# Even steps for a float64 conversion, split weight loads and another order of quad weights in an attention + two-MoE kernel on one core

## The chip, the cores and the metric

One core of one Trainium2 chip runs the whole program. The metric is the device time of one execution in microseconds (us); of several executions the median counts. Before the change three runs gave 1294.26, 1291.40 and 1289.12 us, median 1291.4 us.

## What is computed

Three layers, all in float32 (the weights of the last one come in as float64):

```python
k_p, v_p = mean over 8 keys of k, v                  # 72 pooled keys per head
x = softmax(q @ k_p.T / 8) @ v_p                     # 4 x 8 heads, 576 queries, 64 wide
x = x as (2304, 512)
out = sum over e < 4 of p[:, e] * (relu(x @ w1[e]) @ w2[e])          # w1: 512 x 1024
xn = out / rms(out) * rms_g
y = (silu(xn @ w_gate) * (xn @ w_val)) @ w_out       # 512 x 1536, 1536 x 512, float64 in
```

Every product is built from three fp32r matmuls: each operand is split into a high part (a copy rounded to fp32r) and a low part (the rest), and high x high, high x low and low x high are summed. Over 2 x 2 blocks the products use seven block products instead of eight, so weights and activations need sums and differences of blocks too.

## The kernel before

**Quads.** The unit of work is a *quad*: `quad` (L431) makes four 128-row blocks of hidden values for 768 tokens. It has seven steps (`STEPS`), each of 6 matmuls 128x384 on banks qX, qY, qZ (L462 to L464). After most steps ScalarE copies a bank out (`s`, L470, or `qZ`, L467) or VectorE adds one to `u` (L472, L474). Bank qX is used by steps 0, 2, 4 and 6: step 2 waits for the copy `qZ` after step 0, step 4 for the copy `s` after step 2, step 6 for `u` (L474) after step 4.

**Stages.** There are three passes of 16 MoE quads (kind `m`), then three passes of 12 gate/value quads (kinds `g` and `v` in turn). In this document quad 0 is the first MoE quad, quad 47 the last, quad 48 the first gate quad. The second MoE product (`second`, matmuls 128x512 into `py`, L787 to L789) and the output product (`gx`, `gy`) are threaded between the steps as units.

**The hook.** After each step `hook(n, ...)` is called with the step's number and emits, in this order: the evacuations, the side units, one piece of the next quad's weight preparation (`prep_w`), activations for the next stage (`next_x_ops`), `tick()`, and one step of the background conversion (`next(bg[0])`) unless attention work takes this hook. Everything is emitted in program order into in-order queues (the schedule is manual), so an instruction that waits holds up all that stands behind it on its engine. All DMAs but a few at the start are issued from SP's queue.

**Puts.** `put(dst, src)` (L234) does not issue a store at once: it is issued by the `tick` two hooks later.

**Weights of a quad.** In the first pass over a layer's weights `load_w` (L244) loads the raw blocks into tag `rw` (value quads: `rw2`), and `prep_w` (L254) makes `wr` (three raw blocks, high and low) and `wt` (four sums) with POOL, ScalarE and VectorE, and stores both to DRAM. In later passes `prep_w` only loads `wr` (768 KB) and `wt` (1024 KB) back, L264 and L265, at hook 0 of the quad before. Steps 0, 5 and 6 use `wr` (step 0 only its first block), steps 1 to 4 `wt`. All tags have one buffer unless said otherwise. Tag `rw2` is also the home of the tile `xt` (`xr["s2"]`), which the last quads of MoE pass 3 need for the activations of the first gate pass; its last reader is L207.

**Conversion.** `convert_all` (L326) runs in MoE passes 2 and 3 as the background task: 36 pieces of 128x512 float64 values are loaded as two words each (`cr`), turned into float32 by six VectorE integer operations (`ca`, L367 to L376), one ScalarE copy (`cx`, L369) and two POOL operations (L378, L379), and stored to `wc_d` (24 gate and value pieces) or, for `w_out`, two pieces at a time, combined into eight operands (`combine`, L383) and stored to `ws_d`. `cx` alternates between tag `rw2` and a buffer of the attention pool (`vr`), `cr` between `rw` and `kr`; the two integer arrays `a` and `m` are one tile on tag `tw`. `halt[0]` stops it in the last four quads of a pass.

The places that the prediction's steps touch: `prep_w` around the boundary of quads 47, 48 and 49; the body of `convert_all`; L264/L265.

Of the kernel before, what the change touches and what calls it, by code (L numbers as in the profile page):

```python
# [26 lines left out]
P = 128  # L27
# [11 lines left out]
G = 2  # L39
# [15 lines left out]
def tile_kernel(ctx: ExitStack, tc, qp, kp, vp, dp, w1r, w2r, w64, rg, out):  # L55
    nc = tc.nc
    ctx.enter_context(tc.manual_schedule())
    main = ctx.enter_context(tc.tile_pool(name="main", bufs=1))
    dram = ctx.enter_context(tc.tile_pool(name="dram", bufs=1, space=bass.MemoryType.DRAM))

    def f32(ap):
        return ap.bitcast(F32)
# [169 lines left out]
    puts, clock = [], [0]  # L232

    def put(dst, src):  # L234
        puts.append((clock[0] + 2, dst, src))
# [8 lines left out]
    def load_w(i):  # L244
        if i >= NQ or quads[i][1]:
            return
        k, p, e, r = quads[i]
        t = main.tile([P, 4, 256], F32, name="rw", tag="rw2" if k == "v" else "rw")
        src = w1r[e, r] if k == "m" else wc_d[KINDS.index(k), r]
        nc.sync.dma_start(t.rearrange("p s n -> p (s n)"), src)  # L250
        raw[i] = t

    def prep_w(i):
# [27 lines left out]
        if k == "m":  # L281
            load_w(i + 1)
# [43 lines left out]
    def convert_all():  # L326
# [17 lines left out]
        load(0)  # L344
        yield True
        yield True
        for n, (k, r_, c) in enumerate(keys):
            stop = halt[0]
            if n not in crs:
                load(n)  # L350
                yield True
# [12 lines left out]
            if k < 2:  # L364
                yield True
# [4 lines left out]
            nc.vector.scalar_tensor_tensor(a, hw, 0x80000000, a, op0=ALU.bitwise_and, op1=ALU.bitwise_or)  # L370
            yield True

            mi = m.bitcast(I32)
            nc.vector.tensor_scalar(mi, mi, float(897 << 20), -1.0, op0=ALU.is_ge, op1=ALU.mult)
            nc.vector.scalar_tensor_tensor(a, a, 0x40000000, m, op0=ALU.bitwise_xor, op1=ALU.bitwise_and)
            nc.vector.tensor_scalar(m, a, 0xFF800000, None, op0=ALU.bitwise_and)  # L376

            nc.gpsimd.tensor_tensor(x, x, m.bitcast(F32), op=ALU.mult)  # L378
            nc.gpsimd.tensor_tensor(x, a.bitcast(F32), x, op=ALU.add)  # L379
            if k < 2:  # L380
                put(wc_d[k, r_, :, c * 512:(c + 1) * 512], x)
            else:
                halves[c] = x  # L383
                spare[c] = xt[:, 512:].bitcast(F32R).rearrange("p (a n) -> p a n", a=2)
                if c:
                    yield from combine(r_, halves, spare)
            yield not stop

    def combine(r, halves, spare):
# [12 lines left out]
        def high(t, src):  # L402
            nc.scalar.activation(t[:, 0], src, AF.Copy)

        def low(t, src, n):
            nc.vector.tensor_tensor(t[:, 1], src, f32(t[:, 0]), op=ALU.subtract)
            put(ws_d[r // G, n // 2, :, n % 2, r % G], f32(t))
# [16 lines left out]
        high(t[2], src[2])  # L424
        yield True
        low(t[2], src[2], 2)
        high(t[3], src[3])
        high(t[4], src[4])
        yield True
        low(t[3], src[3], 3)  # L430
        low(t[4], src[4], 4)  # L431
        high(t[6], src[6])
        yield True
        low(t[6], src[6], 6)
# [767 lines left out]
    for si, ((moe, p), ids) in enumerate(stages):  # L1202
# [3 lines left out]
        for i in ids:  # L1206
# [6 lines left out]
            def hook(n, u, v, x):  # L1213
# [18 lines left out]
                halt[0] = i in ids[-4:]  # L1232
# [107 lines left out]
```

## Time and profile before

| | |
|---|---|
| median of three runs | 1291.4 us (1289.12 to 1294.26) |
| the profiled execution, its own time | 1290.88 us |
| its span, first to last instruction | 1289.0 us |
| PE busy / PE weight load busy | 1250.3 us (97%) / 1154.3 us (90%) |
| VectorE / ScalarE / POOL busy | 814.9 / 534.8 / 269.2 us |
| DMA traffic | 339.15 MB, 263 GB/s mean |

The profile says of each engine how long it worked and, before an instruction that started after a pause, what ended the pause. Matmuls are pipelined, so "busy" of PE includes their overlap; the start-to-start distance of two matmuls tells the rate. The span is 1.9 us shorter than the execution's own time.

### The profile page before, as it was taken

The numbers are of one execution on the slowest core, as the hardware profiler recorded it, in microseconds if no ns is written. First come the engines' busy times: TensorE is split into PE (matmuls) and PEld (weight loads), VectorE is DVE, ScalarE is ACT, GpSimd is POOL, SyncE is SP. The second block draws the span as 40 slices with busy tenths as digits, with TensorE's granted clock in tenths as the row PEclk, the third lists the DMA queues.
The fourth block names the chain that finished last, engine by engine and source line by source line (L and its number), as shares of the span: only waits on it lengthen the run. The fifth ranks groups of instructions, "written<-read, shape, count | busy, mean of one in ns | idle before, by whom it ended". The sixth has DMA issues, their size and how long they took to land. (4 is left out here: it accounts for less than half of the span.)

```text
span 1289.0 us, 18313 instructions
## 1 busy us (share of the span) xinstructions
PE 1250.3 (97%) x6872; PEld 1154.3 (90%) x6872; DVE 814.9 (63%) x1340; ACT 534.8 (41%) x1239; POOL 269.2 (21%) x253
## 2 busy tenths in 40 slices
PE   7899999999999999999999999989999999999998
PEld 6788888889888898888988898878999999999998
DVE  5865565557466566544777786465667765786575
ACT  5664444444453333323433342254554433433331
POOL 5335333410032222100342432022220000000000
PEclk8899999999999999999999999989999999999999
DMA  8297777868877777564888997647877776867571
GB/s 245 85 341 275 273 255 257 296 218 322 304 252 283 284 282 266 212 237 175 338 289 313 346 332 264 268 172 257 335 262 276 272 294 234 316 239 303 218 281 50
DMA packets 96537, 339.15 MB, mean 263 GB/s; under 512 B 9408, under 2 KB 32960, under 8 KB 77248
## 3 DMA queue, kind: packets, MB, share of 16 engines
q1 hardware_dynamic: 96112, 336.80, 71.5%
q10 hardware_dynamic: 336, 1.18, 0.3%
q8 instruction: 54, 0.88, 0.3%
q14 instruction: 35, 0.29, 0.1%
HBM read 233.61 MB, written 104.33 MB: 262 GB/s over the span
## 5 line engine op out<-in xcount | busy, mean ns | idle before, releaser
L799 DVE SCALAR_TENSOR_TENSOR y<-py,dps,y 128x512 f32<-128x512 f32 x126 | 94.4, 749 | 183.9 <-PE py L789 183.7
L378 POOL TENSOR_TENSOR cx<-cx,ca 128x512 f32<-128x512 f32 x36 | 48.9, 1357 | 379.1 <-DVE ca L376 127.7
L462 PE MATMUL qX<-xos,wt 128*128 128x384 f32 x336 | 116.9, 348 | 10.4 <-ACT s L470 7.7
L464 PE MATMUL qX<-xos,wt 128*128 128x384 f32 x336 | 114.1, 339 | 0.0
L463 PE MATMUL qX<-xos,wt 128*128 128x384 f32 x336 | 113.7, 338 | 0.0
L789 PE MATMUL py<-w,hB 128*128 128x512 f32 x288 | 113.5, 394 | 0.0
L789 PE MATMUL py<-w,hA 128*128 128x512 f32 x288 | 113.4, 394 | 0.0
L788 PE MATMUL py<-w,hB 128*128 128x512 f32 x288 | 113.3, 393 | 0.0
L788 PE MATMUL py<-w,hA 128*128 128x512 f32 x288 | 113.2, 393 | 0.0
L787 PE MATMUL py<-w,hB 128*128 128x512 f32 x288 | 112.1, 389 | 0.3 <-DVE y L799 0.3
L787 PE MATMUL py<-w,hA 128*128 128x512 f32 x288 | 112.0, 389 | 0.0
L491 ACT ACTIVATE hB<-u 128x768 fp32r<-128x768 f32 x48 | 40.8, 849 | 138.1 <-DVE u L474 138.0
L271 POOL TENSOR_TENSOR tw<-rw 128x512 f32<-128x512 f32 x28 | 40.6, 1449 | 274.7 <-DVE wt L289 173.5
L470 ACT ACTIVATE s<-qX 128x384 f32<-128x384 f32 x85 | 41.6, 489 | 115.0 <-PE qX L464 114.9
L467 ACT ACTIVATE qZ<-qX 128x384 f32<-128x384 f32 x83 | 39.8, 480 | 117.1 <-PE qX L464 83.2
L472 DVE TENSOR_TENSOR u<-qY,s 128x384 f32<-128x384 f32 x84 | 46.6, 554 | 64.3 <-PE qY L464 30.6
L462 PEld LDWEIGHTS qX<-xos,wt 128*128 128x128 f32 x336 | 63.6, 189 | 18.9 <-ACT s L470 10.0
L463 PEld LDWEIGHTS qX<-xos,wt 128*128 128x128 f32 x336 | 63.7, 190 | 2.9
L789 PEld LDWEIGHTS py<-w,hB 128*128 128x128 f32 x288 | 54.0, 188 | 11.5
L789 PEld LDWEIGHTS py<-w,hA 128*128 128x128 f32 x288 | 54.0, 188 | 11.4
L464 PEld LDWEIGHTS qX<-xos,wt 128*128 128x128 f32 x336 | 63.6, 189 | 0.2 <-DVE wt L289 0.2
L787 PEld LDWEIGHTS py<-w,hB 128*128 128x128 f32 x288 | 54.1, 188 | 10.3 <-DVE y L799 0.7
(188 smaller groups left out, 3487.4 us busy)
## 6 DMA issues: line engine op xcount, KB each, us to landing
wt<-wt_d SPq DMA_DIRECT2D x56, 1024.0 KB, 8.2
wr<-wr_d SPq DMA_DIRECT2D x56, 768.0 KB, 6.3
w<-w_d SPq DMA_DIRECT2D x32, 1024.0 KB, 9.3
wt_d<-wt SPq DMA_DIRECT2D x28, 1024.0 KB, 7.3
wr_d<-wr SPq DMA_DIRECT2D x28, 768.0 KB, 5.8
cr<-w SPq DMA_DIRECT2D x36, 512.0 KB, 5.4
w<-ws_d SPq DMA_DIRECT2D x18, 1024.0 KB, 5.4
w_d<-w SPq DMA_DIRECT2D x16, 1024.0 KB, 10.5
```

Of the source, the lines that this page charges most:

```text
L271: nc.gpsimd.tensor_tensor(t[:, T1:N3 + 1], r[:, B12:B12 + 1].to_broadcast([P, 2, 256]), r[:, B11:B22 + 1], op=sub)
L378: nc.gpsimd.tensor_tensor(x, x, m.bitcast(F32), op=ALU.mult)
L462: nc.tensor.matmul(bank[b], wh, xh, start=first and k == 0, stop=False, **kw)
L463: nc.tensor.matmul(bank[b], wh, xl, start=False, stop=False, **kw)
L464: nc.tensor.matmul(bank[b], wl, xh, start=False, stop=k == 1, **kw)
L470: nc.scalar.activation(s[n], bank[b], AF.Copy)
L472: nc.vector.tensor_tensor(u[:, 0], bank["Y"], s[2], op=ALU.add)
L491: nc.scalar.activation(h[:, 0], u, AF.Relu)
L787: nc.tensor.matmul(ps, lhs[0], w[:, 0, c], start=j == 0, stop=False)
L788: nc.tensor.matmul(ps, lhs[0], w[:, 1, c], start=False, stop=False)
L789: nc.tensor.matmul(ps, lhs[1], w[:, 0, c], start=False, stop=j == len(units) - 1)
L799: nc.vector.scalar_tensor_tensor(y_t[t], ps, gate, y_t[t], op0=ALU.mult, op1=ALU.add)
```

## The change

It has four parts. (1) In `convert_all` the work of a piece is spread over three steps with two VectorE operations each; the integer array `a` alternates between tag `tw` and a new buffer `ca` of the attention pool, and `m` moves into the unused half of the piece's `cx` tile; the next load into a buffer is emitted at the end of the piece that read it (`load(n + 2)`), with two loads at a start; the stores of converted data wait three hooks instead of two. (2) In `combine` the same operations stand in six parts instead of seven. (3) In later passes `wr` is loaded as two DMAs, its first block before `wt` and the other two behind it. (4) Value quads keep their raw weights in `rw` and gate quads but the first in `rw2`, and around the first gate quad the load of quad 49 is emitted after quad 48's L279 instead of at the end of its preparation. The conversion is halted half a quad later.

```diff
-    def put(dst, src):
-        puts.append((clock[0] + 2, dst, src))
+    def put(dst, src, steps=2):
+        puts.append((clock[0] + steps, dst, src))
...
-        t = main.tile([P, 4, 256], F32, name="rw", tag="rw2" if k == "v" else "rw")
+        t = main.tile([P, 4, 256], F32, name="rw", tag="rw2" if k == "g" and r else "rw")
...
-            nc.sync.dma_start(wrf, wr_d[n])
+            d = wr_d[n].rearrange("p (a s n) -> p a s n", a=2, s=3)
+            nc.sync.dma_start(f32(wr)[:, :, :1], d[:, :, :1])
             nc.sync.dma_start(wtf, wt_d[n])
+            nc.sync.dma_start(f32(wr)[:, :, 1:], d[:, :, 1:])
...
-        if k == "m":
+        if k == "m" or quads[i - 1][0] == "m":
             load_w(i + 1)
...
         if k != "m":
-            if quads[i - 1][0] == "m":
-                load_w(i + 1)
             load_w(i + 2)
...
-            if not stop:
-                load(n + 1)
             r = crs.pop(n)
             lw, hw = r[:, :, 0], r[:, :, 1]
-            am = main.tile([P, 2, 512], U32, name="ca", tag="tw")
-            a, m = am[:, 0], am[:, 1]
             if n % 2:
+                a = sba.tile([P, 512], U32, name="ca", tag="ca")
                 xt = sba.tile([P, 1024], F32, name="cx", tag="vr")
             else:
+                a = main.tile([P, 1024], U32, name="ca", tag="tw")[:, :512]
                 xt = main.tile([P, 1024], F32, name="cx", tag="rw2")
-            x = xt[:, :512]
-            if k < 2:
-                yield True
+            x, rest = xt[:, :512], xt[:, 512:]
+            m = rest.bitcast(U32)
...
+            if not halt[0]:
+                load(n + 2)
             if k < 2:
-                put(wc_d[k, r_, :, c * 512:(c + 1) * 512], x)
+                put(wc_d[k, r_, :, c * 512:(c + 1) * 512], x, 3)
...
-            yield not stop
+            yield n + 1 in crs
...
-                halt[0] = i in ids[-4:]
+                halt[0] = i in ids[-3:] or i == ids[-4] and n >= 3
```

Three places where instructions move. First SP's queue at the boundary from the MoE to the gate quads; `rw<-wc_d` are raw weights of gate and value quads, in the order of quads 48, 49, 50 and on, `wr_d`/`wt_d<-` the stores of prepared weights. Before:

```order
L250 DMA rw_7490<-wc_d_73 128x1024
L315 DMA w2_7523<-w2_d_76 128x2048
L315 DMA w2_7644<-w2_d_76 128x2048
L241 DMA wr_d_74<-wr_7588 128x1536
L250 DMA rw_7725<-wc_d_73 128x1024
L250 DMA rw_7727<-wc_d_73 128x1024
L241 DMA wt_d_75<-wt_7589 128x2048
L241 DMA wr_d_74<-wr_7740 128x1536
```

The same place in the changed kernel:

```order
L250 DMA rw_7522<-wc_d_73 128x1024
L315 DMA w2_7555<-w2_d_76 128x2048
L315 DMA w2_7676<-w2_d_76 128x2048
L250 DMA rw_7702<-wc_d_73 128x1024
L241 DMA wr_d_74<-wr_7620 128x1536
L250 DMA rw_7759<-wc_d_73 128x1024
L241 DMA wt_d_75<-wt_7621 128x2048
L241 DMA wr_d_74<-wr_7772 128x1536
```

Quad 49's load (the second `rw`) has moved ahead of quad 48's store of `wr` and no longer stands beside quad 50's; quad 50's keeps its place.

Second, VectorE's queue in quad 28, the last conversion pieces of pass 2 (`sm`, `es` are attention). Before:

```order
L990 TENSOR_TENSOR es_4503<-es_4503,sm_4502 128x576
L799 SCALAR_TENSOR_TENSOR y_3298<-py_4597,dps_70,y_3298 128x512
L367 TENSOR_SCALAR ca_4614<-cr_4526 128x512
L368 TENSOR_SCALAR ca_4614<-cr_4526 128x512
L370 SCALAR_TENSOR_TENSOR ca_4614<-cr_4526,ca_4614 128x512
L472 TENSOR_TENSOR u_4571<-qY_4588,s2_4622 128x384
L799 SCALAR_TENSOR_TENSOR y_3298<-py_4637,dps_70,y_3298 128x512
L374 TENSOR_SCALAR ca_4614<-ca_4614 128x512
```

The same place in the changed kernel:

```order
L990 TENSOR_TENSOR es_4516<-es_4516,sm_4515 128x576
L799 SCALAR_TENSOR_TENSOR y_3305<-py_4611,dps_70,y_3305 128x512
L365 TENSOR_SCALAR ca_4625<-cr_4486 128x512
L366 TENSOR_SCALAR cx_4626<-cr_4486 128x512
L370 SCALAR_TENSOR_TENSOR ca_4625<-cr_4486,ca_4625 128x512
L372 TENSOR_SCALAR cx_4626<-cx_4626 128x512
L472 TENSOR_TENSOR u_4584<-qY_4602,s2_4636 128x384
L799 SCALAR_TENSOR_TENSOR y_3305<-py_4650,dps_70,y_3305 128x512
```

The order around `u` is nearly the same; `ca` and `cx` are now buffers that the piece before does not use, and the second operation writes into `cx`.

Third, SP's queue in MoE pass 3, where the first two pieces of `w_out` are combined (`ws_d` stores; `yl`, `xs_d` belong to the norm; `w2` are MoE weights). Before:

```order
L241 DMA ws_d_77<-oh_6042 128x512
L341 DMA cr_6181<-w64 128x1024
L241 DMA ws_d_77<-oh_6044 128x512
L837 DMA yl_6218<-y_d_78 128x512
L341 DMA cr_6234<-w64 128x1024
```

In the changed kernel, where `cr_6048` is the load of the piece that `cr_6181` holds above, and `cr_5978` that of the piece before it:

```order
L341 DMA cr_5978<-w64 128x1024
L265 DMA wr_6005<-wr_d_74 128x2x256
L266 DMA wt_6006<-wt_d_75 128x2048
L267 DMA wr_6005<-wr_d_74 128x2x512
L837 DMA yl_6042<-y_d_78 128x512
L341 DMA cr_6048<-w64 128x1024
L315 DMA w2_6069<-w2_d_76 128x2048
L88 DMA xs_d_72<-st_6040 256x1x128 x2
L241 DMA ws_d_77<-cx_5935 128x512
```

The raw piece is requested ahead of the stores of the pieces before it, a whole group of stores earlier, and each load of `wr` is two.

## Rows read from the trace of the kernel before

**Rows 1.** The page's engine row, and the granted clock in 40 slices (tenths).
```profile
PE 1250.3 (97%) x6872; PEld 1154.3 (90%) x6872; DVE 814.9 (63%) x1340; ACT 534.8 (41%) x1239; POOL 269.2 (21%) x253
...
PEclk8899999999999999999999999989999999999999
```

**Rows 2.** PE's instructions in order of time around the first gate quad: start, duration, instruction, [idle before <-releaser].
```profile
853.65 0.34 PE L464 MATMUL qY<-xoa,wt 128*128 128x384 f32 x1
859.09 0.69 PE L462 MATMUL qX<-xos,wt 128*128 128x384 f32 x1 [5.10 <-ACT s L470]
859.57 0.53 PE L463 MATMUL qX<-xos,wt 128*128 128x384 f32 x1
859.89 0.53 PE L464 MATMUL qX<-xos,wt 128*128 128x384 f32 x1
...
862.77 0.41 PE L464 MATMUL qZ<-xoa,wr 128*128 128x384 f32 x1
...
864.58 0.33 PE L462 MATMUL qX<-xoa,wr 128*128 128x384 f32 x1
864.75 0.33 PE L463 MATMUL qX<-xoa,wr 128*128 128x384 f32 x1
```

**Rows 3.** The same stretch on SP, ACT and DVE.
```profile
839.23 0.95 DVE L279 TENSOR_TENSOR wr<-rw,wr 128x768 fp32r<-128x768 f32 x1
...
852.35 0.96 DVE L207 TENSOR_TENSOR xr<-xr,xt 128x768 f32<-128x768 f32 x1
853.37 0.80 SPq L250 DMA_DIRECT2D rw<-wc_d  x2
857.08 0.84 ACT L277 ACTIVATE wr<-rw 128x768 fp32r<-128x768 f32 x1 [5.13 <-DMA rw<-wc_d]
857.83 0.83 ACT L170 ACTIVATE xos<-xr 128x768 fp32r<-128x768 f32 x1
858.57 0.47 ACT L470 ACTIVATE s<-qX 128x384 f32<-128x384 f32 x1
```

**Rows 4.** Windows: length, PE, PEld, DVE, ACT, POOL busy (instructions), granted clock, DMA share, GB/s.
```profile
858.00:860.00 2.00, 0.91 (x3) 0.91 (x4) 2.00 (x2) 1.98 (x4) 1.84 (x3) 0.50 0.97 401
```

**Rows 5.** PE in order of time: every wait of PE in the conversion's stretch but one of 0.35 us.
```profile
535.15 0.45 PE L462 MATMUL qX<-xos,wr 128*128 128x384 f32 x1 [1.71 <-DVE u L474]
...
663.60 0.44 PE L462 MATMUL qX<-xos,wt 128*128 128x384 f32 x1 [1.22 <-ACT s L470]
...
691.79 0.44 PE L462 MATMUL qX<-xos,wt 128*128 128x384 f32 x1 [1.08 <-ACT qZ L467]
694.70 0.44 PE L462 MATMUL qY<-xoa,wt 128*128 128x384 f32 x1 [1.59 <-ACT s L470]
...
784.77 0.44 PE L462 MATMUL qX<-xos,wr 128*128 128x384 f32 x1 [0.81 <-DVE u L474]
```

**Rows 6.** DVE and ACT in order of time: the conversion's own waits.
```profile
529.51 0.43 DVE L367 TENSOR_SCALAR ca<-cr 128x512 uint32<-128x512 uint32 x1 [2.17 <-POOL cx L379]
...
686.28 0.43 DVE L367 TENSOR_SCALAR ca<-cr 128x512 uint32<-128x512 uint32 x1 [4.01 <-DMA cr<-w]
...
662.49 0.67 ACT L369 ACTIVATE cx<-cr 128x512 f32<-128x512 uint32 x1 [4.95 <-DMA wc_d<-cx]
```

**Rows 7.** One VectorE operation beside a POOL operation, and alone.
```profile
634.10 1.63 POOL L379 TENSOR_TENSOR cx<-ca,cx 128x512 f32<-128x512 f32 x1
634.49 2.05 DVE L494 SCALAR_TENSOR_TENSOR hB<-u,hB 128x768 fp32r<-128x768 f32 x1
...
650.11 0.95 DVE L494 SCALAR_TENSOR_TENSOR hB<-u,hB 128x768 fp32r<-128x768 f32 x1
```

**Rows 8.** Waits of PE, whole run: us in total, times, longest.
```profile
PE qY L462 <- DMA wt<-wt_d: 2.5, 3, 1.1
```

**Rows 9.** The page's DMA issues: count, KB each, us from issue to landing.
```profile
wt<-wt_d SPq DMA_DIRECT2D x56, 1024.0 KB, 8.2
wr<-wr_d SPq DMA_DIRECT2D x56, 768.0 KB, 6.3
```

More of the change, by code (lines that the diff above doesn't have):

```diff
@@ L344, in convert_all @@
         load(0)
+        load(1)
         yield True
@@ L347, in convert_all @@
         for n, (k, r_, c) in enumerate(keys):
-            stop = halt[0]
             if n not in crs:
                 load(n)
+                load(n + 1)
                 yield True
                 yield True
-            if not stop:
-                load(n + 1)
             r = crs.pop(n)
             lw, hw = r[:, :, 0], r[:, :, 1]
-            am = main.tile([P, 2, 512], U32, name="ca", tag="tw")
-            a, m = am[:, 0], am[:, 1]
             if n % 2:
+                a = sba.tile([P, 512], U32, name="ca", tag="ca")
                 xt = sba.tile([P, 1024], F32, name="cx", tag="vr")
             else:
+                a = main.tile([P, 1024], U32, name="ca", tag="tw")[:, :512]
                 xt = main.tile([P, 1024], F32, name="cx", tag="rw2")
-            x = xt[:, :512]
-            if k < 2:
-                yield True
+            x, rest = xt[:, :512], xt[:, 512:]
+            m = rest.bitcast(U32)
             nc.vector.tensor_scalar(a, hw, 3, 0x7FFFFFFF, op0=ALU.logical_shift_left, op1=ALU.bitwise_and)
@@ L369, in convert_all @@
             nc.scalar.activation(x, lw, AF.Copy, scale=2.0 ** -52)
+            yield True
             nc.vector.scalar_tensor_tensor(a, hw, 0x80000000, a, op0=ALU.bitwise_and, op1=ALU.bitwise_or)
-            yield True
             mi = m.bitcast(I32)
             nc.vector.tensor_scalar(mi, mi, float(897 << 20), -1.0, op0=ALU.is_ge, op1=ALU.mult)
+            yield True
             nc.vector.scalar_tensor_tensor(a, a, 0x40000000, m, op0=ALU.bitwise_xor, op1=ALU.bitwise_and)
@@ L379, in convert_all @@
             nc.gpsimd.tensor_tensor(x, a.bitcast(F32), x, op=ALU.add)
+            if not halt[0]:
+                load(n + 2)
             if k < 2:
-                put(wc_d[k, r_, :, c * 512:(c + 1) * 512], x)
+                put(wc_d[k, r_, :, c * 512:(c + 1) * 512], x, 3)
             else:
                 halves[c] = x
-                spare[c] = xt[:, 512:].bitcast(F32R).rearrange("p (a n) -> p a n", a=2)
+                spare[c] = rest.bitcast(F32R).rearrange("p (a n) -> p a n", a=2)
                 if c:
                     yield from combine(r_, halves, spare)
-            yield not stop
+            yield n + 1 in crs
     def combine(r, halves, spare):
@@ L406, in low @@
             nc.vector.tensor_tensor(t[:, 1], src, f32(t[:, 0]), op=ALU.subtract)
-            put(ws_d[r // G, n // 2, :, n % 2, r % G], f32(t))
+            put(ws_d[r // G, n // 2, :, n % 2, r % G], f32(t), 3)
         src = (a11, a12, sm[:, 0], sm[:, 1], sm[:, 2], a22, sm[:, 3], a21)
@@ L424, in combine @@
         high(t[2], src[2])
+        high(t[3], src[3])
         yield True
         low(t[2], src[2], 2)
-        high(t[3], src[3])
+        low(t[3], src[3], 3)
         high(t[4], src[4])
-        yield True
-        low(t[3], src[3], 3)
-        low(t[4], src[4], 4)
         high(t[6], src[6])
         yield True
+        low(t[4], src[4], 4)
         low(t[6], src[6], 6)
```

## The prediction

> **What bounds the kernel now.** Read the page's engine row first [rows 1]: PE is busy 1250.3 of 1289.0 us. No matmul is added or taken away, so the change can only win pauses of PE, at most 38.7 us, and stretches in which PE ran at a lower clock. The clock row of the 40 slices [rows 1] shows such a stretch at the start, which the change does not touch, and one more, in the 27th slice (838 to 870 us). Then ask PE's waits, in order of time, three questions: which pauses lie in the code that the diff touches, what ended each, and who held that one up.
>
> There are three places. (a) At 859.09 PE sat idle 5.10 us for a ScalarE copy `s` [rows 2]. It is step 4 of quad 48, the first gate quad. (b) Six pauses in the stretch of the conversion, five of them shown [rows 5]: 1.71, 1.22, 1.08, 1.59 and 0.81 us, and one of 0.35; together 6.76 us. (c) Three waits for `wt<-wt_d` in the later gate passes, 2.5 us in all, the longest 1.1 us [rows 8].
>
> **Part by part: quad 49's raw weights.** ScalarE stood still for 5.13 us before L277 at 857.08, waiting for `rw<-wc_d`; it was ready at 857.08 - 5.13 = 851.95 [rows 3]. Behind L277 in its in-order queue stand L170 (0.83 us) and then the copy `s` for which PE waited. The load itself was issued at 853.37, right after L207 ended (852.35 + 0.96 = 853.31), because before the change quad 49's raw tile is in `rw2`, where L207 still reads `xt` [rows 3]. So this is a buffer wait, and the 3.7 us from 853.37 to 857.08 are the transfer.
>
> After the change quad 49 uses `rw`, which is free when quad 48's L279 (839.23 + 0.95 = 840.2) has read it [rows 3], and SP's queue has the load at that place. Even with the 8.2 us of a transfer twice as large [rows 9] it lands at 848.4, before ScalarE is ready at 851.95. The wait of 5.10 us goes. What is late next? L277 now runs at about 852; L170 still needs L207's result of 853.31 and ends at 854.14; the copy `s` (0.47 us) ends at 854.6. PE could go on at 853.65 + 0.17 = 853.8 [rows 2]. So 0.8 us of the wait stays.
>
> The clock: the granted clock was 0.50, the lower of its two levels (1.2 of 2.4 GHz), from the pause on [rows 4]. Matmuls started 0.32 us apart (859.57 to 859.89) where later they start 0.17 us apart (864.58 to 864.75) [rows 2]. From 859.09 to 862.77 that lost 3.68 x (1 - 0.17/0.32) = 1.7 us. With a pause of 0.8 us in place of 5.1 I expect no drop, since shorter pauses elsewhere, up to 2 us [rows 5], go with full-speed slices [rows 1].
>
> Sum for (a): 5.1 + 1.7 - 0.8 = **6.0 us** won. Bounds: 6.8 if no wait stays; 4.0 if quad 50 is late. Its load still waits for L207, is issued at 853.4 and by the same 3.7 us lands at 857.1; quad 49 starts three steps of 6 x 0.17 = 1.0 us after 854.6, at 857.7, and asks for it one step later. Some 2 us of slack, and the two stores behind it in SP's queue are not ahead of it.
>
> **The conversion.** Three different holds made the six pauses. At 529.51 VectorE waited 2.17 us for POOL to finish with the only `ca` tile [rows 6]; `u` stands behind it and PE then waited 1.71 us [rows 5]. At 686.28 VectorE waited 4.01 us for the raw piece, whose load was asked for too late [rows 6]; 1.08 and 1.59 us of PE follow. At 662.49 ScalarE waited 4.95 us for a store from the buffer that it was to write, and PE 1.22 us for the copy behind it [rows 5, 6]. The change removes the first (two buffers for `a`, `m` beside its own `cx`) and the second (loads a whole piece earlier, ahead of the stores in SP's queue). It does not remove the third. A store is now issued three hooks after its piece, and a gate or value piece writes the same buffer again four hooks after, not five; a step more is only given to `w_out`. Besides, `m` now lies in the `cx` tile, so VectorE too waits for that store, with `u` and the adds of `y` behind it.
>
> The new waits, bounded: nothing, if SP runs far enough ahead to issue the store as soon as POOL is done; or, for the ten reuses in MoE pass 3 (five of gate and value pieces, five of `w_out` pairs), each the price of the one before, 1.22 us of PE, which is 12.2. In pass 2 attention takes hooks between, and the distance is five hooks or more. I take 3.0, two or three payments: a wait of 4.95 us of ScalarE cost PE only a quarter of that [rows 5, 6], so most will go unpaid. Gain for (b): 6.8 - 3.0 = **3.8 us**, bounds 6.8 and -5.4. The six parts of `combine` and the halt half a quad later change no instruction count; I cost them at nothing, covered by VectorE, which is busy 63% of the span [rows 1].
>
> A VectorE operation beside POOL is slow: 2.05 us instead of 0.95 [rows 7]. Before, VectorE often stood still while POOL worked on the piece; now it works. That would give back up to 1.1 us of a 2.17 us wait, and it belongs to the 3.0 above. The Trainium skill says this as a rule against the change (GPSIMD Engine Reference, Specifications): POOL shares its SBUF interfaces with VectorE and contends with its operations that read two SBUF inputs. The row agrees; by that rule half of what the separate buffers win would be lost, some 1 us of PE.
>
> **The split load.** `wt` has 256 KB ahead of it instead of 768. The rows give 8.2 - 6.3 = 1.9 us for its 1024 KB [rows 9], so it lands about 1.0 us earlier. Three waits of at most 1.1 us shrink to nearly nothing: 2.3 of 2.5 us. The last part of `wr` is needed four steps after `wt`, so its later end is hidden. There are 56 more DMAs in SP's queue, and rows of 6 KB are cut to 1 and 2 KB; no row shows that price. Bounds: +2.5 and, by the rival below, a loss. I take **2.0 us**, near the rows.
>
> The swap of `rw` and `rw2` in the rest of the first gate pass exchanges two equal buffers: nothing.
>
> **Sum.** 6.0 + 3.8 + 2.0 = 11.8 us; 1290.88 - 11.8 = 1279.1 us. The profiled execution is 0.5 us below the median of 1291.4, well within the runs' own spread of 5.1 us; I predict **1279 us**.
>
> **Rivals.**
> (1) The conversion's waits only change their names: the late stores and POOL beside VectorE cost PE all of the 6.8 us. For it: ScalarE's 4.95 us wait, of the kind that becomes more frequent. Against: raw pieces and `ca` are surely free earlier. 1290.9 - 6.0 - 2.0 = 1283 us.
> (2) The boundary's wait comes back: quad 50's load, or ScalarE's queue with its table load, holds quad 49 as long as quad 48 was held. For: the slack of 2 us is short. Against: only 512 KB are asked for there, where before 1024 KB landed in 3.7 us. 1290.9 - 5.8 = 1285 us.
> (3) Slower: the three-part weight load. If a transfer goes by the number of contiguous pieces and not by bytes, `wt` lands after three pieces per partition instead of two, at 8.2 x 3/2 = 12.3 us, 4.1 us later, in 24 gate quads of 7 x 1.0 = 7 us each, three of which already wait. Even 1 us of it left on PE in each quad is 24 us: 1290.9 - 9.8 + 24 = 1305 us. It decides from 0.4 us per quad on (9.8 / 24). Against: a 6.3 us landing for 768 KB and 8.2 us for both together follow bytes, not pieces. The Trainium skill has a rule that speaks for this rival (DMA: Bandwidth & Descriptors, Measured): batch DMAs to 1 MiB or more for 75% of peak. No run here shows what a load of 256 KB in pieces of 1 KB costs.
> (4) The change does not do what it says, because other holds stand behind each wait at once: 1291 us.
>
> **How the numbers follow.** A measurement of this kernel can tell 0.5%, 6.5 us, from no change; that is faster below 1284.9. Chances: the forecast 0.70; rival (1) 0.14, of which 0.10 below that line; (2) 0.07; (3) 0.04; (4) 0.05. Faster 0.70 + 0.10 = 0.80; same 0.04 + 0.07 + 0.05 = 0.16; slower 0.04. Range: all gains whole are 6.8 + 6.8 + 2.5 = 16.1, 1274.8, and 2 us for the spread of runs, 1273; at the other end 4.0 from the boundary alone, 1287, which takes in rivals (1) and (2).
>
> **What would show it.** In PE's waits 5.10 is gone and at most 1 us stands at step 4 of quad 48; the 27th slice of the clock row reads 9; quad 49's raw load is issued about 13 us before quad 50's. VectorE's L365 waits neither for POOL nor for a raw piece; what is left of conversion waits stands at L366 and L369, for stores. The wait for `wt` is below 0.5 us. I am wrong if PE's waits between 600 and 800 us exceed 6 us, if a wait for `wr` or `wt` appears in most gate quads, or if the clock still drops after 850 us.

## The result, and the profile after

The changed kernel takes 1276.55 us, the median of four runs (1276.34 to 1279.73), against 1291.16 us for the kernel before (four runs, 1289.12 to 1294.26). The ratio is 0.9891, 95% interval 0.9865 to 0.9916: 14.6 us or 1.1% faster, where 11.8 us were predicted. The profiled execution took 1276.43 us, its span is 1274.1 us, 14.9 us shorter than before.

The page of the changed kernel: engine row, granted clock in 40 slices, DMA packets, two rows of its DMA issues (count, KB each, us from issue to landing).

```profile
PE 1247.5 (98%) x6872; PEld 1153.5 (91%) x6872; DVE 828.2 (65%) x1340; ACT 535.4 (42%) x1239; POOL 268.7 (21%) x253
...
PEclk8899999999999999999999999999999999999999
...
DMA packets 118937, 339.15 MB, mean 266 GB/s; under 512 B 10304, under 2 KB 48192, under 8 KB 99648
...
wt<-wt_d SPq DMA_DIRECT2D x56, 1024.0 KB, 7.4
wr<-wr_d SPq DMA_DIRECT2D x56, 512.0 KB, 8.0
```

Against [rows 1] the 27th slice of the clock reads 9 instead of 8, and VectorE is busy 13.3 us longer with the same number of instructions. `wt` lands 0.8 us sooner than in [rows 9]; the row of `wr` is now its later part.

PE itself gives landmarks: some short pauses stand in both traces at the same matmul. They cut the span into stretches that hold one part of the change each. The **conversion stretch** runs from the first pause of this kind (135.08 in both traces) to step 2 of quad 48, which starts after a pause of 0.20 us for `qZ` (851.61 before, 845.44 after). The **boundary** runs from there to the next pause on `qY` for `s` (891.80 and 880.29). Then 112.1 us in both traces. The **gate stretch** runs from a pause of 0.59 us for `s` (1003.87 and 992.38) to the last pause of `gy` for `y` (1278.57 and 1263.67).

| | conversion stretch | boundary | gate stretch |
|---|---|---|---|
| before | 716.53 us | 40.19 | 274.70 |
| after | 710.36 | 34.85 | 271.29 |
| won | 6.17 | 5.34 | 3.41 |
| predicted | 3.8 | 6.0 | 2.0 |

The three sum to 14.92 us, the whole gain of the span; 11.8 were predicted.

**Boundary.** PE of the changed kernel in order of time:

```profile
847.46 0.34 PE L464 MATMUL qY<-xoa,wt 128*128 128x384 f32 x1
849.04 0.44 PE L462 MATMUL qX<-xos,wt 128*128 128x384 f32 x1 [1.25 <-ACT s L470]
849.32 0.33 PE L463 MATMUL qX<-xos,wt 128*128 128x384 f32 x1
849.49 0.34 PE L464 MATMUL qX<-xos,wt 128*128 128x384 f32 x1
```

The same stretch on the other engines:

```profile
843.56 1.94 POOL L273 TENSOR_TENSOR tw<-rw 128x512 f32<-128x512 f32 x1 [20.01 <-DVE wt L291]
...
845.20 1.12 DVE L174 TENSOR_TENSOR xoa<-xr,xoa 128x768 fp32r<-128x768 f32 x1
...
845.58 1.34 POOL L276 TENSOR_TENSOR tw<-rw,tw 128x256 f32<-128x256 f32 x1
845.67 0.85 ACT L279 ACTIVATE wr<-rw 128x768 fp32r<-128x768 f32 x1
846.35 1.38 DVE L207 TENSOR_TENSOR xr<-xr,xt 128x768 f32<-128x768 f32 x1
...
847.76 0.84 ACT L170 ACTIVATE xos<-xr 128x768 fp32r<-128x768 f32 x1 [1.25 <-DVE xr L207]
847.80 0.32 SPq L250 DMA_DIRECT2D rw<-wc_d  x1
848.51 0.47 ACT L470 ACTIVATE s<-qX 128x384 f32<-128x384 f32 x1
```

And its windows (columns as in [rows 4]):

```profile
849.00:850.00 1.00, 0.96 (x5) 0.96 (x6) 1.00 (x3) 0.98 (x2) 0.00 (x0) 1.00 0.78 229
```

The wait for quad 49's raw weights is gone (L279 here is L277 of [rows 3]): ScalarE runs it at 845.67 without a wait. PE's pause of 5.10 us [rows 2] is 1.25 us. The granted clock right behind it is 1.00 (2.4 GHz) where it was 0.50 (1.2 GHz) [rows 4], and matmuls follow 0.17 us apart. What is late next is L207, as predicted, but by more: ScalarE waits 1.25 us for it with L170, and the copy `s` stands behind L170. L207 took 1.38 us instead of 0.96: POOL now prepares quad 49 at this time, and L207 ends 0.81 us after POOL's L276 (845.58 + 1.34 = 846.92).

**Conversion.** PE's pauses in the conversion's own stretch are four, 2.10 us together, where six made 6.76 [rows 5]:

```profile
534.04 0.44 PE L462 MATMUL qX<-xos,wr 128*128 128x384 f32 x1 [0.39 <-DVE u L474]
...
629.33 0.44 PE L462 MATMUL qX<-xos,wt 128*128 128x384 f32 x1 [0.87 <-ACT s L470]
...
651.14 0.45 PE L462 MATMUL qX<-xos,wr 128*128 128x384 f32 x1 [0.60 <-DVE u L474]
...
791.87 0.44 PE L462 MATMUL qX<-xos,wr 128*128 128x384 f32 x1 [0.24 <-DVE u L474]
```

The conversion's waits in the changed kernel, 330 to 830 us (us in total, times, longest); the ScalarE copy that the prediction calls L369 is L367 here:

```profile
ACT cx L367 <- DMA wc_d<-cx: 11.9, 6, 3.9
...
DVE ca L365 <- DMA cr<-w: 9.4, 2, 4.9
DVE cx L366 <- DMA wc_d<-cx: 6.9, 3, 4.5
```

L365 does not wait for POOL any more; for a raw piece it waits twice (the prediction said never), at the first piece of either pass, with no pause of PE behind it. What is left is the third hold, the store from the same buffer, on both engines. Two of PE's pauses follow it: VectorE or ScalarE waited (3.91 us at L367, 4.51 us at L366), `s` or `u` stood behind.

One reason that there is more of this waiting than before is the stores' own time, from issue to landing; here before and then after the change (count, KB each, us):

```profile
wc_d<-cx SPq DMA_DIRECT2D x24, 256.0 KB, 2.2
```

```profile
wc_d<-cx SPq DMA_DIRECT2D x24, 256.0 KB, 7.3
```

In MoE pass 3 all five stores of the changed kernel are issued 0.02 to 0.03 us after POOL's last operation on the piece, so it was not their issue that was late, but their landing.

**Gate stretch.** The three waits of PE for `wt` [rows 8] are gone.

### The profile page after: what moved, and what is told of

It is laid out like the page before. It is cut to its first block, busy times and chain, and to the rows that moved or that the text cites. A ratio compares the mean times of both kernels' runs of the same rounds, so it can differ in the third digit from the quotient of the medians.

```text
span 1274.1 us, 18396 instructions
## 1 busy us (share of the span) xinstructions
PE 1247.5 (98%) x6872; PEld 1153.5 (91%) x6872; DVE 828.2 (65%) x1340; ACT 535.4 (42%) x1239; POOL 268.7 (21%) x253
## 4 chain that ended last, share of the span: by engine, by line
PE 84%; DVE 8%; DMA 4%; ACT 2%; issue 1%; SPq 0%; DVEq 0%; ACTq 0%
PE py L788 9%; PE py L789 9%; PE py L787 9%; PE qX L462 8%; PE qX L464 8%; PE qX L463 8%; PE qY L462 4%; PE qY L463 4%; PE qY L464 4%; PE qZ L462 2%; PE qZ L464 2%; PE qZ L463 2%; DMA wc_d<-cx 2%; PE gy L734 1%; PE gx L667 1%; PE av L1020 1%
## 5 line engine op out<-in xcount | busy, mean ns | idle before, releaser
L377 POOL TENSOR_TENSOR cx<-cx 128x512 f32<-128x512 f32 x36 | 49.8, 1383 | 380.4 <-DVE cx L376 91.2
L462 PE MATMUL qX<-xos,wt 128*128 128x384 f32 x336 | 116.2, 346 | 5.1 <-ACT s L470 3.5
L464 PE MATMUL qX<-xos,wt 128*128 128x384 f32 x336 | 113.6, 338 | 0.0
L462 PEld LDWEIGHTS qX<-xos,wt 128*128 128x128 f32 x336 | 63.3, 188 | 13.2 <-ACT s L470 5.8
L789 PEld LDWEIGHTS py<-w,hB 128*128 128x128 f32 x288 | 54.0, 188 | 11.5
L789 PEld LDWEIGHTS py<-w,hA 128*128 128x128 f32 x288 | 54.0, 188 | 11.4
L464 PEld LDWEIGHTS qX<-xos,wt 128*128 128x128 f32 x336 | 63.1, 188 | 0.2 <-DVE wt L291 0.2
L788 PEld LDWEIGHTS py<-w,hA 128*128 128x128 f32 x288 | 54.0, 188 | 10.1
```

What stands on the lines that cost most here:

```text
L462: nc.tensor.matmul(bank[b], wh, xh, start=first and k == 0, stop=False, **kw)
L464: nc.tensor.matmul(bank[b], wl, xh, start=False, stop=k == 1, **kw)
L788: nc.tensor.matmul(ps, lhs[0], w[:, 1, c], start=False, stop=False)
L789: nc.tensor.matmul(ps, lhs[1], w[:, 0, c], start=False, stop=j == len(units) - 1)
```

## The experiments

The runs fall into three groups, e1 to e4, e5 to e8 and e9 to e12, each on one chip beside the kernel before (medians 1292.95, 1292.45 and 1292.08 us). Diffs are against the changed kernel. Ratios are to the kernel before, with the 95% interval; the stretches are those above, from each run's trace.

| run | median us | ratio | conversion | boundary | gate |
|---|---|---|---|---|---|
| e1_conversion_old | 1286.23 | 0.9947 (0.9928 to 0.9966) | 718.64 | 34.87 | 271.25 |
| e2_wr_whole | 1279.93 | 0.9906 (0.9886 to 0.9925) | 709.55 | 34.88 | 274.92 |
| e3_quad_weights_old | 1283.71 | 0.9932 (0.9915 to 0.9949) | 711.01 | 41.25 | 271.25 |
| e4_wr_cut_in_place | 1284.44 | 0.9938 (0.9920 to 0.9957) | 713.07 | 34.88 | 276.56 |
| e5_new_tags_late_load | 1279.04 | 0.9898 (0.9883 to 0.9912) | 713.18 | 34.83 | 271.23 |
| e6_one_integer_tile | 1281.62 | 0.9915 (0.9899 to 0.9931) | 716.14 | 34.85 | 272.01 |
| e7_load_one_ahead | 1280.28 | 0.9907 (0.9886 to 0.9929) | 714.52 | 34.85 | 271.46 |
| e8_stores_two_hooks | 1276.30 | 0.9880 (0.9863 to 0.9897) | 710.55 | 34.86 | 271.58 |
| e9_change_again | 1278.06 | 0.9891 (0.9875 to 0.9906) | 711.36 | 34.84 | 271.88 |
| e10_s4_later | 1279.67 | 0.9908 (0.9896 to 0.9921) | 710.52 | 34.83 | 272.78 |
| e11_split_gate_only | 1278.67 | 0.9895 (0.9881 to 0.9908) | 711.43 | 34.89 | 271.32 |
| e12_three_together | 1275.99 | 0.9872 (0.9859 to 0.9886) | 709.22 | 34.83 | 271.26 |

Five traces have the change's conversion and its loads unaltered ahead of quad 48's step 2: after, e3, e5, e9 and e10. Their conversion stretch is 710.36 to 713.18 us. So 2.8 us there are the spread of one trace, and a smaller effect can't be read from it. What lies ahead of this stretch, which no edit touches, takes 134.22 to 137.52 us in the traces; it is in the medians and not in the stretches. The boundary and the gate stretch (without a wait for `wt`) repeat within 0.1 us and 0.4 us.

### The boundary: e3, e5, e10

e3 undoes part (4):

```diff
-        ...tag="rw2" if k == "g" and r else "rw")
+        ...tag="rw2" if k == "v" else "rw")
...
-        if k == "m" or quads[i - 1][0] == "m":
+        if k == "m":
             load_w(i + 1)
...
+            if quads[i - 1][0] == "m":
+                load_w(i + 1)
             load_w(i + 2)
```

> The changed kernel with value quads' raw weights in rw2 again and the load of quad 49 emitted at the end of quad 48's preparation. Theory (buffer wait at the boundary): the pause of 5.1 us at step 4 of quad 48 and a granted clock of 0.50 for some 6 us are back, +5.3 us, 1281.9 us; nothing else moves. Rival (the conversion's new pace made the boundary earlier and shares in the gain): a pause of 3 us or less.

PE of e3 (L464 to L466 are L462 to L464 of the others), and its window after the pause:

```profile
853.99 0.69 PE L464 MATMUL qX<-xos,wt 128*128 128x384 f32 x1 [5.46 <-ACT s L472]
854.47 0.52 PE L465 MATMUL qX<-xos,wt 128*128 128x384 f32 x1
854.79 0.52 PE L466 MATMUL qX<-xos,wt 128*128 128x384 f32 x1
```

```profile
854.00:858.00 4.00, 4.00 (x13) 4.00 (x14) 3.38 (x6) 2.83 (x4) 2.05 (x2) 0.50 1.02 410
```

The pause and the half clock come back together, the boundary is 41.25 us, 6.4 us longer than after, and the other stretches stay. It is even 1.1 us longer than before the change: the pause is 5.46 us instead of 5.10, and matmuls stay 0.32 us apart for 5.3 us behind it instead of 3.7. Part (4) is shown to be the cause.

e5 keeps the new tags and puts quad 49's load back to its old place in program order:

```diff
-        if k == "m" or quads[i - 1][0] == "m":
+        if k == "m":
             load_w(i + 1)
...
+            if quads[i - 1][0] == "m":
+                load_w(i + 1)
             load_w(i + 2)
```

> The changed kernel with the new buffers for raw weights, but the load of quad 49 emitted at the end of quad 48's preparation, as before. Theory (what held the load was the buffer that xt still used): the load is issued before 849 us, lands before ScalarE asks for it at about 846 plus its queue, the pause at step 4 stays below 2.5 us and the time within 1.5 us of 1276.6. Rival (what held it was its place in SP's queue): the pause is 4 us or more and the clock drops, 1281.9 us.

SP of e5; the row holds the issues of quads 49 and 50, which stand next to each other again:

```profile
838.53 13.63 SPq L250 DMA_DIRECT2D rw<-wc_d  x2
```

The boundary is 34.83 us, as after. Quad 49's issue is 10.96 us ahead of step 2's start (849.49 in this run); in the changed kernel, at 834.08 of 845.44, it is 11.36 us ahead. The place in the queue is worth 0.4 us of lead and no time; quad 50's issue waits behind it until 838.53 + 13.63 = 852.16. e3 and e5 differ in the buffers alone, by 6.4 us at the boundary. The buffer was the whole matter.

e10 was to move quad 48's L170 behind the copy `s`, so that the copy need not wait for L207:

```diff
+        if not early:
+            yield
```

> The changed kernel with the high part of s4 (L170) emitted one hook later at the boundary, so that the copy s that PE waits for stands ahead of it on ScalarE. Theory (the 1.25 us left of the boundary's wait is L170 waiting for L207 ahead of the copy): the pause at step 4 of quad 48 falls below 0.3 us and step 4 to the next landmark does not get longer, about 1.2 us faster than the changed kernel. Rival (s4 is needed at step 6 and is now late there): a new pause of 0.5 us or more at step 6 of quad 48, no gain.

It missed its place: at this boundary the activations are made with `early` set, and the order did not change; the added step acts only between MoE passes 1 and 2. The pause is 1.22 us and the boundary 34.83. That L170's wait for L207 makes the rest of the pause stands on the rows above alone; it wasn't tried. The run serves as a repeat, and it is 1279.67 us (1279.15 to 1283.23) beside e9's 1278.06: in its trace a wait for `wt` of 1.21 us was back.

### The conversion: e1, e6, e7, e8

e1 puts the whole conversion of the kernel before into the changed kernel (parts (1) and (2) undone, about 40 lines; the core):

```diff
-                a = sba.tile([P, 512], U32, name="ca", tag="ca")
...
+            am = main.tile([P, 2, 512], U32, name="ca", tag="tw")
+            a, m = am[:, 0], am[:, 1]
...
-                load(n + 2)
...
+                load(n + 1)
...
-                put(wc_d[k, r_, :, c * 512:(c + 1) * 512], x, 3)
+                put(wc_d[k, r_, :, c * 512:(c + 1) * 512], x)
```

> The changed kernel with the conversion (pieces, integer tile, loads, combine, halt) as it was before; the new quad-weight order and the split loads stay. Theory (the landmark count: PE is 6.2 us earlier at step 2 of quad 48, and all of it comes from the conversion): about 1276.6 + 6.2 = 1282.8 us, step 2 of quad 48 again near 851.6 us, the pauses of 1.71, 1.22, 1.08, 1.59 us back, while the pause at step 4 of quad 48 stays near 1.2 us and no wait for wt comes back. Rival (split loads, which also run in MoE passes 2 and 3, give a part of the 6.2 by landing earlier): step 2 of quad 48 between 846 and 850 us and a time below 1281.

PE of e1, four of its ten pauses in the stretch:

```profile
536.94 0.44 PE L462 MATMUL qX<-xos,wr 128*128 128x384 f32 x1 [1.71 <-DVE u L474]
...
693.56 0.44 PE L462 MATMUL qX<-xos,wt 128*128 128x384 f32 x1 [1.48 <-ACT qZ L467]
696.48 0.44 PE L462 MATMUL qY<-xoa,wt 128*128 128x384 f32 x1 [1.60 <-ACT s L470]
...
788.46 0.44 PE L462 MATMUL qX<-xos,wr 128*128 128x384 f32 x1 [1.42 <-DVE u L474]
```

The pauses of [rows 5] are back at the same places. The stretch is 718.64 us, 5.5 to 8.3 us above the five traces of the change's conversion. The median is 3.4 us above the 1282.8 that were expected: in its trace the time ahead of the stretch is 1.7 us longer than before the change (136.82 against 135.08) and the stretch 2.1 us longer (716.53), less than the spread above.

e6 takes the second integer buffer away:

```diff
-                a = sba.tile([P, 512], U32, name="ca", tag="ca")
+                a = main.tile([P, 1024], U32, name="ca", tag="tw")[:, :512]
```

> The changed kernel with the integer array a of every piece on the one tag tw (m stays beside cx). Theory (VectorE's wait for POOL made part of the pauses): L365 waits for POOL again some 2 us in ten or more pieces, pauses of PE of 1 to 2 us in all come back, 1278 to 1279 us. Rival (late raw pieces alone made the pauses): within 0.5 us of the changed kernel at step 2 of quad 48 (845.4 us). Second rival (the loads and waits combine): 1280 us or more.

VectorE of e6, and PE behind it:

```profile
527.07 0.43 DVE L376 TENSOR_SCALAR cx<-ca 128x512 uint32<-128x512 uint32 x1
530.33 0.43 DVE L365 TENSOR_SCALAR ca<-cr 128x512 uint32<-128x512 uint32 x1 [2.83 <-POOL cx L378]
```

```profile
536.51 0.44 PE L462 MATMUL qX<-xos,wr 128*128 128x384 f32 x1 [1.79 <-DVE u L474]
```

The first hold is back, pause included, with POOL waits at L365 of 38.4 us in 20 pieces (none after). The stretch is 716.14 us, 3.0 us above the largest of the five. Some 1.5 of them (an estimate: three us at half the clock) are the clock: from 537.50 to 540.50, behind this pause, the granted clock is 0.50. So one buffer more is worth 3 us or more in the new order of work. How much of the gain over the old conversion it makes can't be read from this run: the new order with one buffer waits for POOL more than the old one did, 38.4 us in 20 pieces against 21.6 us in 11.

e7 loads one piece ahead, at the end of the step, as before:

```diff
-        load(1)
...
+            stop = halt[0]
...
+            if not stop:
+                load(n + 1)
...
-            if not halt[0]:
-                load(n + 2)
...
-            yield n + 1 in crs
+            yield not stop
```

> The changed kernel with raw pieces asked for at the start of the piece before, one at a time, as before the change. Theory (late raw pieces made the pauses around 691 us and 784 us): VectorE or ScalarE wait for cr again up to 4 us, PE's pauses of 1 to 2.7 us come back, 1278 to 1280 us. Rival (separate integer buffers alone removed the pauses): step 2 of quad 48 within 0.5 us of 845.4 us and no pause over 1 us between 600 and 800 us.

VectorE waits for raw pieces in e7, 330 to 830 us (L366 is L365 after), and its two long PE pauses:

```profile
DVE ca L366 <- DMA cr<-w: 17.4, 5, 5.3
```

```profile
630.93 0.61 PE L461 MATMUL qX<-xos,wt 128*128 128x384 f32 x1 [1.99 <-ACT s L469]
...
655.65 0.44 PE L461 MATMUL qX<-xos,wr 128*128 128x384 f32 x1 [1.98 <-DVE u L473]
```

Three more waits for raw pieces, of 4.19 us at most, and none has a pause of PE right behind it; the two long pauses follow waits for stores, as after, only longer. The stretch of 714.52 us is 1.3 us above the five. But behind the first of these pauses the granted clock fell (windows as in [rows 4]):

```profile
631.00:633.00 2.00, 2.00 (x7) 2.00 (x8) 1.63 (x4) 0.44 (x1) 0.20 (x1) 0.51 0.97 400
```

Matmuls are 0.32 us apart there up to 634.21, which cost some 1.6 us (ten of them at 0.15 us more). The long pauses that the theory named are back, but not behind raw pieces. A gain from loading further ahead is not shown; VectorE's wait of 4.01 us at 686.28 [rows 6] is only 1.86 us in this run, so what the second hold cost by itself stays open.

e8 issues the stores two hooks after their piece, as before:

```diff
-                put(wc_d[k, r_, :, c * 512:(c + 1) * 512], x, 3)
+                put(wc_d[k, r_, :, c * 512:(c + 1) * 512], x)
...
-            put(ws_d[r // G, n // 2, :, n % 2, r % G], f32(t), 3)
+            put(ws_d[r // G, n // 2, :, n % 2, r % G], f32(t))
```

> The changed kernel with the conversion's stores issued two hooks after the piece instead of three. Theory of the prediction (late stores hold the next writer of the same buffer; 3 us were put down for that, two pauses of 0.87 and 0.60 us are in the trace): waits of L366 and L369 for stores shrink, step 2 of quad 48 up to 1 us earlier, 1275.5 us. Rival (SP stands at the store until POOL is done and holds up the loads behind it, which is why three hooks are better): longer waits for cr or wr, 1277.5 us or more.

The waits of e8 for these stores, 330 to 830 us:

```profile
ACT cx L367 <- DMA wc_d<-cx: 7.2, 3, 3.4
...
DVE cx L366 <- DMA wc_d<-cx: 3.1, 2, 1.8
```

They fall from 11.9 and 6.9 us (the same 24 stores land in 5.0 us instead of 7.3), and PE does not gain: the stretch is 710.55 us, with other pauses (1.14 and 0.91 us) in place of those at 629 and 651. The third hook is neither a gain nor a loss that can be measured (ratio 0.9880 against 0.9891, intervals overlap).

### The split load: e2, e4, e11

e2 loads `wr` whole ahead of `wt`, as before:

```diff
-            d = wr_d[n].rearrange("p (a s n) -> p a s n", a=2, s=3)
-            nc.sync.dma_start(f32(wr)[:, :, :1], d[:, :, :1])
+            nc.sync.dma_start(wrf, wr_d[n])
             nc.sync.dma_start(wtf, wt_d[n])
-            nc.sync.dma_start(f32(wr)[:, :, 1:], d[:, :, 1:])
```

> The changed kernel with wr loaded as one DMA ahead of wt again. Theory (order of bytes): the three waits for wt of 1.14, 0.83 and 0.56 us come back in the gate passes with what PE loses around each, about +3.4 us, 1280.0 us; nothing changes before 850 us. Rival (the cut costs something in the MoE passes that is hidden in the sum): PE is earlier than in the changed kernel at step 2 of quad 48 (845.44 us) by 0.5 us or more, and the net is below +2 us.

e4 cuts it in two and leaves both parts ahead of `wt`:

```diff
-            nc.sync.dma_start(wtf, wt_d[n])
             nc.sync.dma_start(f32(wr)[:, :, 1:], d[:, :, 1:])
+            nc.sync.dma_start(wtf, wt_d[n])
```

> The changed kernel with wr cut into the same two DMAs, but both ahead of wt: the cut without the new order. Theory (order of bytes alone wins, the cut costs next to nothing): as with wr whole, about 1280.0 us, waits for wt between 0.5 and 1.5 us in three or four quads. Rival (transfers go by pieces, so the cut costs): waits for wt in more than six gate quads or longer than 2 us, 1284 us or more. Second rival (the earlier start of the first small piece is what helps, not the place of wt): 1277 us.

PE's waits for `wt` in e2, then in e4:

```profile
997.51 0.44 PE L460 MATMUL qY<-xos,wt 128*128 128x384 f32 x1 [0.81 <-DMA wt<-wt_d]
...
1042.81 0.44 PE L460 MATMUL qY<-xos,wt 128*128 128x384 f32 x1 [0.88 <-DMA wt<-wt_d]
...
1175.97 0.44 PE L460 MATMUL qY<-xos,wt 128*128 128x384 f32 x1 [1.12 <-DMA wt<-wt_d]
```

```profile
1003.87 0.44 PE L462 MATMUL qY<-xos,wt 128*128 128x384 f32 x1 [1.08 <-DMA wt<-wt_d]
...
1050.20 0.44 PE L462 MATMUL qY<-xos,wt 128*128 128x384 f32 x1 [1.89 <-DMA wt<-wt_d]
...
1183.69 0.44 PE L462 MATMUL qY<-xos,wt 128*128 128x384 f32 x1 [1.44 <-DMA wt<-wt_d]
```

e2's gate stretch is 274.92 us, that of before. Step 2 of quad 48 came at 843.77, 1.67 us earlier than after, as its rival said; 0.86 of that lies ahead of the conversion stretch. In e4 the same three waits are longer, 4.4 us against 2.8, and the stretch is 276.56, 1.6 us longer than e2's. So the cut alone costs 1.6 us there, in the three quads that wait and in no other; `wt` behind 256 KB instead of 768 wins 276.56 - 271.29 = 5.3 us, and the two together 3.6. The median of e4 is 4.5 us above that of e2, in the range of the rival though its sign (more quads, or longer waits) did not come. Its conversion stretch is 3.5 us longer than e2's, where PE waits for no weights; why is open.

e1, e2 and e4 had suggested that the cut costs time in the MoE passes. e11 splits in the gate passes only:

```diff
+            if k == "m":
+                nc.sync.dma_start(wrf, wr_d[n])
+                nc.sync.dma_start(wtf, wt_d[n])
+            else:
...
```

> The changed kernel with wr loaded whole in the MoE passes and in two parts only in the gate passes. Theory (the cut costs something where DMA is busiest, MoE pass 3, and wins only in the gate passes): step 2 of quad 48 1 to 2 us earlier than in the changed kernel on this chip, no wait for wt, 1 to 2 us faster. Rival (what the runs with whole wr showed before 850 us was the spread of that stretch): within 0.5 us of the changed kernel.

Raw pieces land in 5.3 us there, as before the change (5.4), where the change has 7.1 us. But the conversion stretch is 711.43 us against 711.36 in e9, and the median 1278.67 us against 1278.06. PE does not see the later landing here, and the gain that was expected did not come. A cost below the spread stays possible: three traces with the change's pieces and whole `wr` in the MoE passes (e2, e11, e12) have 709.22 to 711.43 us, the five above 710.36 to 713.18.

### The repeat, and a combination: e9, e12

e9 is the changed kernel once more, without an edit, as the measure for its group.

> The changed kernel once more, as the measure on the same chip for the three that follow and for how much its own pauses between 600 and 850 us differ from execution to execution. Theory (that stretch depends on when transfers land): first shown pause near 630 us between 0.5 and 2.5 us, step 2 of quad 48 between 710 and 714 us after the first pause of quad 2 at 135 us; the gate passes repeat to 0.2 us. Rival (the stretch repeats too, and the 2.5 us pause of the run with the late load came from that edit): 710.4 us as in the first trace.

1278.06 us (1277.93 to 1278.59), ratio 0.9891 as at first. Its trace has one wait for `wt`, which shows what a pause costs:

```profile
1174.87 0.33 PE L463 MATMUL qX<-xoa,wr 128*128 128x384 f32 x1
1175.04 0.34 PE L464 MATMUL qX<-xoa,wr 128*128 128x384 f32 x1
1175.71 0.44 PE L462 MATMUL qY<-xos,wt 128*128 128x384 f32 x1 [0.33 <-DMA wt<-wt_d]
1175.99 0.33 PE L463 MATMUL qY<-xos,wt 128*128 128x384 f32 x1
```

The idle time is listed as 0.33 us, but without it the next matmul would have started at 1175.04 + 0.17 = 1175.21: it started 0.50 us late. The one after it followed by 0.28 us instead of 0.17, which makes 0.61. The gate stretch, 271.88 us, is 0.6 us longer than those without a wait.

e12 joins e11's split, e8's stores and e10's edit (which does nothing at the boundary):

```diff
+            if k == "m":
+                nc.sync.dma_start(wrf, wr_d[n])
+                nc.sync.dma_start(wtf, wt_d[n])
+            else:
...
-                put(wc_d[k, r_, :, c * 512:(c + 1) * 512], x, 3)
+                put(wc_d[k, r_, :, c * 512:(c + 1) * 512], x)
```

> The two edits above together, and the conversion's stores two hooks after the piece. Theory (the gains add, the store's delay is worth nothing): 2 to 3 us faster than the changed kernel. Rival (earlier stores make SP stand and hold up the loads of wr behind them): a wait for wr or wt in the MoE passes and no more gain than the better of the two alone.

1275.99 us (1274.69 to 1276.52) beside e9's 1278.06 on the same chip: 2.1 us less, and the two sets of runs don't overlap, though the intervals of their ratios do. It has the shortest conversion stretch of all, 709.22 us, and no wait for `wt`. It is the fastest kernel here, by little. Which of its edits makes the 2.1 us is not shown: alone, e8's and e11's won nothing that could be measured.

## Why the prediction was right, and which terms were mis-sized

The forecast (1279 us, range 1273 to 1287, faster) held, and in the main by its own mechanisms: each of the three places gave a gain, and no rival came. Three terms were off, by -0.7, +2.4 and +1.4 us, so that their errors in part cancelled.

**(a) Boundary, 6.0 predicted, 5.34 measured.** The wait was a buffer wait (e3, e5) and its end brought the clock back (1.7 expected; from step 4 to the end of the boundary the way shrank from 32.71 to 31.25 us, 1.46). From step 2 to step 4 it won 3.88 us (7.48 to 3.60). The mis-sized step is "0.8 us of the wait stays": 1.25 stayed. The prediction took L207 at its old 0.96 us. With quad 49's weights there, POOL starts on them at once, and L207 runs beside it in 1.38 us; so more than the 1 us that the prediction allowed at step 4 is left. One premise failed: it expected no drop of the clock, since pauses of up to 2 us went with full slices. In e6 and e7 a drop followed pauses of 1.79 and 1.99 us. That the 1.25 us left here brought none is what the trace shows, not what [rows 1] and [rows 5] could tell. Quad 50 was not late; its load was issued at 847.80, 13.7 us behind quad 49's, as predicted.

**(b) Conversion, 3.8 predicted, 6.17 measured.** The waits came as forecast: first and second hold gone but for two starts, third hold left, on both engines. That the old conversion as a whole made the loss is shown (e1); the share of each hold is not (e6, e7). Two sizes were off. The 3.0 us for the late stores were two payments, 0.87 and 0.60 us as listed. The reason given, stores issued a hook later, is not borne out: without the third hook as much pause stays (e8). And the lower bound ("nothing, if SP runs far enough ahead to issue the store as soon as POOL is done") failed, since the stores of pass 3 were issued at once and still held the next writer. The prediction left out their landing, 7.3 us where it had been 2.2. Which part of the change makes them land later is not separated: with the old conversion they take 4.0 us (e1), with stores after two hooks 5.0 (e8), with `wr` whole 5.7 (e2). And the sum took the listed idle time for the cost of a pause; e9 shows some 0.3 us on top of each. With the pauses of other origin the whole stretch had nine listed ones of 7.68 us before and has six of 2.57 after: 5.11 + 3 x 0.3 = 6.0 us, against 6.17 measured. e1 has ten, 9.31 us: by the same count 6.74 + 4 x 0.3 = 7.9 us more than after, measured 8.28. In e6 and e7, where the clock fell too, the count falls short by 1.3 and 1.1 us; in the other traces it is right within 0.7 us.

**(c) Split load, 2.0 predicted, 3.41 measured.** Again the unlisted part: three waits of 2.53 us [rows 8] and 3 x 0.3 make 3.4. No run with the split in the new order has all three back, but one of them remains in some (0.33 us in e9, 0.49 in e6, 1.21 in e10), so "shrink to nearly nothing" is true of most runs, not of all. The step to "1.0 us earlier" was a misreading that came out near: 1024 KB in 1.9 us would be 550 GB/s, more than any window shown here moved (410 GB/s at most), so the two loads must have overlapped and 1.9 us is not the second one's own time. `wt` landed 0.8 us sooner.

**The rivals.** (1), waits that only change their names, is refuted by e1: with the old conversion the stretch is at least 5.5 us longer. (2) is refuted by the boundary of 34.85 us. (3), slower by the number of pieces, is there in kind and small: e4's cut costs 1.6 us in the gate stretch, where the rival needed 0.4 us in each of 24 quads. The profile's DMA packets rise from 96537 (e2 has 96536) to 118937. The Trainium skill (DMA: Bandwidth & Descriptors, Measured) has the rule to batch DMAs to 1 MiB or more; e4 agrees with it in direction. The order of the bytes outweighs the cut here by 5.3 to 1.6 us. (4) falls with the result.

## What to carry to other kernels

When an in-order engine waits for a load, look first at when the load was *allowed* to start: the reader that still holds its buffer decides more than its place in the queue (e5), and the same goes for a scratch tile that two engines pass to and fro (e6). Ask of a store not only when it is issued but when it lands, since its buffer is held until then. Put the bytes that are needed first ahead of those that can wait, even if a load must be cut for it. Count pauses of PE as well as their listed time, and expect that an engine freed from a wait will next run beside another and slow it.

## What the runs showed of the hardware

**A pause of PE costs more than its listed idle time,** here some 0.3 us more: matmuls start 0.17 us apart and are shown for 0.33, so the idle time is counted from an end 0.16 us later than the next start would have been; and the first matmul behind a pause takes 0.28 us to the next one. The Trainium skill (Perfetto Trace Analysis, Tensor Engine Instruction) states that the profile's end of a matmul is worked out, not observed; these rows agree with that.

**VectorE stood still while POOL worked, with one input too.** VectorE and POOL of the changed kernel:

```profile
526.34 0.42 DVE L365 TENSOR_SCALAR ca<-cr 128x512 uint32<-128x512 uint32 x1
526.68 1.51 DVE L366 TENSOR_SCALAR cx<-cr 128x512 uint32<-128x512 uint32 x1
...
528.77 1.12 DVE L370 SCALAR_TENSOR_TENSOR ca<-cr,ca 128x512 uint32<-128x512 uint32 x1
```

```profile
526.56 1.34 POOL L377 TENSOR_TENSOR cx<-cx 128x512 f32<-128x512 f32 x1 [13.11 <-ACT s L470]
527.98 1.36 POOL L378 TENSOR_TENSOR cx<-ca,cx 128x512 f32<-128x512 f32 x1
```

L366 has one tensor input, takes 0.42 us alone (L365) and 1.51 us here: it ends at 528.19, 0.29 us after POOL's operation (527.90). L370, 0.68 us alone, ends 0.55 us after POOL's second one. So VectorE is not slowed in proportion; it waits until POOL's operation is over. Of 36 times each in this trace, L365 is stretched 14 times and L366 11 times, and all 25 end 0.28 to 0.30 us after a POOL operation; seven stretched 128x768 ones (L207, L281, L494; 0.95 us alone) end 0.81 or 0.82 us after one. That is 0.13 to 0.14 us less than their own time, whatever their length. The Trainium skill (SBUF — State Buffer, Who interferes with whom) calls it an exclusive lock, which `tensor_scalar` in a two-port mode takes too; these rows agree. The prediction had counted operations with two inputs only. L365 and L366 are busy for 25.7 and 25.9 us in all, where the same two operations (L367, L368) took 15.2 and 15.1 before: 21.3 us more, which covers VectorE's 13.3 us more of busy time; other operations took less. The pauses of PE behind VectorE's `u` in the changed kernel are 0.24 to 0.60 us, where [rows 5] had 1.71 and 0.81.

**The clock can fall for some three us behind a short pause, and the row of 40 slices does not show it.** Behind pauses of PE of 1.79 us (e6, 536.51) and 1.99 us (e7, 630.93) the granted clock was 0.50 and 0.51 (1.2 GHz) and matmuls were 0.32 us apart; behind pauses of 1.71 us (before, 535.15), 1.98 us (e7, 655.65) and 2.51 us (e5, 632.23) it stayed at 1.00 (2.4 GHz). The length of the pause alone did not decide it. The slices, 32 us each, read 9 in e6 and e7 at these places as everywhere around them.
